# Two gated MLPs after attention: 19 weight quadrants decoded earlier and kept in DRAM, left operands of the second half prepared five steps ahead

## Chip, cores and metric

The kernel runs on one core of a Trainium2 chip. The metric is the device time of one execution in microseconds (us); lower is better.

## What is computed

The inputs are q, k and v of 4 x 12 heads (448 x 64 each), and the weights of two layers. The reference, cut to what matters:

```python
q_n, k_n = rmsnorm(q, g_q), rmsnorm(k, g_k)
scores = np.matmul(q_n, k_n.transpose(0, 1, 3, 2)) / np.sqrt(64)
attn = softmax(scores)                      # with the row maximum taken off
x = heads side by side of attn @ v          # 1792 x 768
x = ((x @ w_a) * (x @ w_b)) @ w_out         # layer 0: 768 -> 1536 -> 768
x = (sigmoid(x @ w_gate) * (x @ w_val)) @ w_out2   # layer 1, same sizes
```

The weights arrive as 64-bit floats, the activations are 32-bit.

## The kernel before

**Matrices in quadrants.** Each matrix product of the two layers is made by a seven-product scheme on a 2 x 2 split (products 1 to 7, `PASSES`): every product needs one left and one right operand that are quadrants or sums and differences of quadrants. Each operand is split into a high and a low part, and each product is three TensorE matmuls (high x high, low x high, high x low).

**Layers in two parts.** `first_part` makes a layer's hidden matrix: 12 blocks of columns m (of w_a and w_b, or w_gate and w_val, in turn) by 7 products p, 84 events (m, p) in the order of the list `orders`, each of 18 matmuls. `second_part` multiplies the gated result with w_out: 7 products by 6 steps f, 42 steps k of 18 matmuls in layer 0. Attention comes first and handles 24 pairs of heads; the first 16 matmul groups of layer 0's first event are mixed into its end (the calls `mlp` in the table `end`, L495).

**Decoding weights.** A weight quadrant comes as 384 KB of 64-bit words into a `raw` tile. `decode` (L633) makes a 128 x 384 tile `d` of 32-bit floats from it: one ScalarE activation (ACT, L639) and three VectorE instructions (DVE, L640, L642, L646). It is a generator with three pauses; after the last instruction it calls `fill`, which issues the load of the next quadrant but one, since two `raw` tiles are kept loaded. `decodes` (L662) walks over a list `plan` of what is to be decoded: "g" entries are the events, four of the seven products of a block need a new quadrant (`NEEDS`); "o" entries are the 24 quadrants of the layer's w_out, which go through tiles d5 and d8 in turn and are stored to DRAM (`wd`), one every 2.3 events from event 24 on. `splits` (L712) forms a product's right operand from the d tiles (L722, L726) and casts it into the tiles wh (ACT, L734) and wl (DVE, L576). `prepare` (L746) advances both generators by one pause per call.

**Who calls prepare.** In attention two calls of `decode` per pair of heads from pair 6 on (L440), each one pause, until the first 8 quadrants and four operands are made. In `first_part` one call per three matmuls, for three events ahead. In the last six steps of layer 0's `second_part` (L1115) for layer 1, whose generator starts with 12 pauses that load four quadrants.

**Left operands.** `operands` (L774) forms the left operands S1 to S4 and A22 of a first part on VectorE (L800, and L576 for xl) and ScalarE (L791 for xh), a piece every 12 matmuls. In the second part `beside` has three generators: `loads` issues the DMAs of gated quadrants (u) and of stored weight quadrants (d), `rights` makes wh and wl (L1026, L1029, L576), `lefts` makes gh and gl (L1044, L1056, L576). Both are kept up to AHEAD = 3 steps ahead of the step that TensorE is given (L1077). The left operands lie in a ring of six tiles.

**Order.** The program order on each engine is the order in which this Python code emits instructions; each engine runs its own list in order. All DMAs named below are issued by the SyncE queue (SP), also in order. A tile name such as d8 with one buffer makes its next writer wait until its last reader, a DMA too, is done.

**Tail of attention.** The table `end` holds, for the last pair (-1) and those before it: x_tr (TensorE transposes into one of three PSUM buffers `tr`), x_out (copies to SBUF, half 0 on ACT, half 1 on DVE, L356 and L358), rsum_tr and rsum_post (the softmax sums through a `tr` buffer and the ACT copy L390 to `row`), the DMAs dr<-row and rs<-dr, norm (L406), put (xd<-xs), and ten calls of `decode` between them.

Of the kernel before, what the change touches and what calls it, by code (L numbers as in the profile page):

```python
# [23 lines left out]
def attention_then_two_gated_mlps(  # L24
# [37 lines left out]
    nc = tc.nc  # L62
# [3 lines left out]
    P = 128  # L66
# [7 lines left out]
    NPAIR = B * NP  # L74
# [11 lines left out]
    HB = DM // 2  # L86
    HF = NF // 2
# [16 lines left out]
    def in_dram(name, cols, *counts):  # L104
        if not counts:
            return dram1.tile([P, cols], F32, tag=name, name=name)
        return [in_dram(f"{name}_{n}", cols, *counts[1:]) for n in range(counts[0])]
# [2 lines left out]
    gd = in_dram("gd", S2, 2, 5, HF)  # L110
    wd = in_dram("wd", HB, 2, 6, HF)
    bd = in_dram("bd", HB, 2, 2, 2)


    def attention():
# [322 lines left out]
            begin_u()  # L438

        def decode(i, n):  # L440
            if i > 5:
                prepare(0, 3, 1)

        def close_s(i):
            sctx.close()
# [84 lines left out]
    AHEAD = 3  # L530
# [3 lines left out]
    EARLY = 4  # L534
# [9 lines left out]
    NS = len(PASSES) * HF  # L544
# [35 lines left out]
        rest(t, hi, lo, eng)  # L580


    def quadrant(l, n, j, q):

        words = layers[l][n].bitcast(U32)
        r, c = q
        if n < 2:
            f = j + HF * c
            return words[HB * r:HB * r + HB, 2 * P * f:2 * P * f + 2 * P].rearrange("(k p) f -> p k f", p=P)
        f = j + HF * r  # L590
        return words[P * f:P * f + P, 2 * HB * c:2 * HB * c + 2 * HB]
# [5 lines left out]
    def weights(l):  # L597

        plan = []
        events = orders[l]  # L600
        k = 0
        for e, (m, p) in enumerate(events):
            plan.append(("g", m, p))
            while k < 4 * HF and e >= 24 + 2.3 * k:
                plan.append(("o", k % HF, (Q11, Q21, Q12, Q22)[k // HF]))
                k += 1
        assert k == 4 * HF
        wanted = [
            (2, m, p) if x == "o" else (m % 2, m // 2, NEEDS[p]) for x, m, p in plan if x == "o" or p in NEEDS
        ]  # L610
        loaded = []
        total = len(wanted)

        def fill():

            while wanted and len(loaded) < (4 if total - len(wanted) < 10 and len(free_u) >= 3 else 2):
                load()

        def load():
            n, j, q = wanted.pop(0)  # L620
            tag = None
            if [t for t, _ in loaded].count(None) >= 2:
                tag, u = take_u()
                r = u[:, 0:2 * HB].bitcast(U32).rearrange("p (f w) -> p f w", w=2)
            else:
                r = rawp.tile([P, HB, 2], U32, tag="raw", name="raw")
            if n < 2:
                nc.sync.dma_start(out=r.rearrange("p (k f) w -> p k (f w)", f=P), in_=quadrant(l, n, j, q))
            else:
                nc.sync.dma_start(out=r.rearrange("p f w -> p (f w)"), in_=quadrant(l, n, j, q))  # L630
            loaded.append((tag, r))

        def decode(t):  # L633
# [27 lines left out]

        def decodes():  # L662
            e = k = -1
            if l == 0:
                fill()
                yield
            else:
                for n in range(12):
                    if n % 3 == 0:
                        load()  # L670
                    yield
            for x, m, p in plan:
                now = stores[:]
                if x == "o":
                    k += 1
                    t = dec("d5" if k % 2 else "d8")
                    yield from decode(t)
                    stores.append((wd[l][QUADS.index(p)][m], t))
                else:
                    e += 1  # L680
                    if p in NEEDS:
                        q = QUADS.index(NEEDS[p])
                        spilled = 2 <= m < EARLY and p < 3
                        tag = f"d{4 * (m % 2) + (q + 1 if spilled else q)}"
                        if q == 1 and m >= EARLY:
                            tag = "d1"
                        if l == 1:
                            while held[0] is not None and tag not in held[0]:
                                yield
                            if held[0] is not None:  # L690
                                held[0].remove(tag)
                        t = dec(tag)
                        B[m, q] = t
                        yield from decode(t)
                        if spilled:
                            stores.append((bd[l][m % 2][q // 2], t))
                for dst, t in now:
                    nc.sync.dma_start(out=dst, in_=t)
                    stores.pop(0)
                decoded[l] = e  # L700
                yield
            for dst, t in stores:
                nc.sync.dma_start(out=dst, in_=t)
            decoded[l] = NE
# [35 lines left out]
        return decodes(), splits()  # L740

    decoded = [-1, -1]

    held = [None]

# [224 lines left out]
    def beside(l):  # L970
# [95 lines left out]
        def step(k, must=False):  # L1066
# [7 lines left out]
                stores()  # L1074
            if len(gl) < 4 and (max(gl) if gl else k) < k + 7:
                next(load, None)
            for d, it in ((WI, right), (GI, left)):  # L1077
                if (max(d) if d else -1) < min(k + AHEAD, NS - 1):
                    next(it, None)

        return step
# [186 lines left out]
```

## Time and profile before

| | us |
|---|---|
| median of 3 runs | 1249.66 (1248.96 to 1249.98) |
| the profiled execution's own time | 1248.36 |
| its span, first to last instruction | 1246.5 |
| TensorE (PE) busy | 1199.8 (96%) |
| VectorE (DVE) busy | 935.9 (75%) |
| ScalarE (ACT) busy | 655.3 (53%) |
| mean granted TensorE clock | 0.991 of full |
| moved by DMA | 203 MB |

Attention takes the stretch to about 284 us, layer 0's first part 284 to 608, its second part 608 to 767, layer 1's first part 768 to 1085, its second part the rest. The views below give each instruction group with its line, its tiles (out<-in) and the time an engine sat idle before it with what it waited for; a stretch of time can be asked for by itself. The time of a matmul is modelled, so two neighbours overlap in the list.

### The profile page before, as it was taken

Reading aid. Unit: us, or ns where it says so; the run is one execution under the profiler, and the core shown is the slowest. Engines: PE = TensorE matmul, PEld = TensorE weight load, DVE = VectorE, ACT = ScalarE, POOL = GpSimd, SP = SyncE. Lnnn points to the kernel's source line nnn. Section 1 sums busy time; section 2 is a strip of 40 time slices with the busy share of each in tenths; the row PEclk is TensorE's granted clock in tenths of the full one; section 3 lists DMA queues with packets and bytes.
Section 4 is the critical chain, followed back from the end, with each engine's and each line's share of the span. In section 5 each row is a group of like instructions: output and inputs, shape, how many; then the busy total and the mean of one; then the engine's idle time right before and its main releaser. Section 6 shows DMA issues by size and latency. Waiting matters only on the chain.

```text
span 1246.5 us, 18142 instructions
## 1 busy us (share of the span) xinstructions
PE 1199.8 (96%) x6414; PEld 1014.0 (81%) x6414; DVE 935.9 (75%) x1621; ACT 655.3 (53%) x1271; POOL 157.0 (13%) x240
## 2 busy tenths in 40 slices
PE   5999999999799999999999999889999999999997
PEld 3666666667688888888888878778888888999997
DVE  6788889874987787876668689966877877557583
ACT  4777787873543544344355556444445344445543
POOL 3656667700000000000000000000000000000000
PEclk9999999999899999999999999999999999999999
DMA  5244455327134565653865753233655654677573
GB/s 130 72 134 127 135 151 160 114 85 253 40 117 148 170 195 153 201 168 113 313 223 160 236 178 119 72 108 119 187 183 161 198 159 155 221 266 252 179 258 101
DMA packets 142025, 202.99 MB, mean 163 GB/s; under 512 B 23240, under 2 KB 116592, under 8 KB 141936
## 3 DMA queue, kind: packets, MB, share of 16 engines
q1 hardware_dynamic: 140496, 201.26, 51.0%
q8 instruction: 50, 0.82, 0.3%
q10 hardware_dynamic: 1440, 0.59, 0.2%
q14 instruction: 39, 0.32, 0.1%
HBM read 147.46 MB, written 54.35 MB: 162 GB/s over the span
## 4 chain that ended last, share of the span: by engine, by line
PE 81%; DVE 10%; ACT 4%; issue 2%; DMA 1%; POOL 1%; ACTq 0%; SPq 0%; DVEq 0%; POOLq 0%
PE mm L887 45%; PE mm L1140 10%; PE mm L1150 9%; PE pv L371 5%; PE s L311 4%; PE tr L342 3%; DVE xl L576 2%; DVE nm L317 2%; PE tr L264 1%; PE tr L339 1%; ACT gh L1056 1%; DVE d L646 1%; DMA d<-wd 1%; DVE wl L576 1%; DVE u L1044 1%
## 5 line engine op out<-in xcount | busy, mean ns | idle before, releaser
L887 PE MATMUL mm<-xh,wh 128*128 128x512 f32 (+1 forms) x1008 | 370.3, 367 | 10.5 <-ACT u L943 4.1
L887 PE MATMUL mm<-xl,wh 128*128 128x512 f32 (+1 forms) x1008 | 370.9, 368 | 5.2 <-DVE xl L576 5.2
L887 PE MATMUL mm<-xh,wl 128*128 128x512 f32 (+1 forms) x1008 | 371.6, 369 | 0.0
L576 DVE TENSOR_TENSOR wl<-d,wh 128x384 fp32r<-128x384 f32 x252 | 140.2, 557 | 158.1 <-ACT wh L734 99.9
L887 PEld LDWEIGHTS mm<-xh,wh 128*128 128x128 f32 x1008 | 190.9, 189 | 36.7 <-ACT u L939 4.5
L887 PEld LDWEIGHTS mm<-xl,wh 128*128 128x128 f32 x1008 | 190.8, 189 | 29.7 <-DVE xl L576 6.9
L887 PEld LDWEIGHTS mm<-xh,wl 128*128 128x128 f32 x1008 | 190.6, 189 | 21.2
L734 ACT CAST wh<-d 128x384 fp32r<-128x384 f32 x168 | 86.1, 513 | 167.8 <-DVE d L722 150.1
L1029 ACT CAST wh<-d 128x384 fp32r<-128x384 f32 x84 | 43.3, 515 | 146.8 <-DVE d L1026 46.5
L639 ACT ACTIVATE d<-raw 128x384 f32<-128x384 f32 x140 | 77.9, 557 | 63.8 <-DMA raw<-in_moe_w_gate_dram 13.9
L329 ACT ACTIVATE P<-s,nm 128x448 f32<-128x448 f32 x168 | 105.3, 636 | 10.3 <-DVE nm L317 9.5
L317 DVE TENSOR_REDUCE nm<-s 128x1 f32<-128x448 f32 x168 | 97.5, 615 | 4.1 <-PE s L311 4.1
L1150 PE MATMUL mm<-wh,gh 128*128 128x384 f32 x294 | 98.8, 336 | 0.6 <-ACT ah L1173 0.3
L1150 PE MATMUL mm<-wl,gh 128*128 128x384 f32 x294 | 98.6, 335 | 0.0
L1150 PE MATMUL mm<-wh,gl 128*128 128x384 f32 x294 | 98.5, 335 | 0.0
L1140 PE MATMUL mm<-gh,wh 128*128 128x512 f32 x252 | 92.6, 367 | 3.1 <-ACT ah L1173 2.9
L1140 PE MATMUL mm<-gl,wh 128*128 128x512 f32 x252 | 93.1, 369 | 0.0
L1140 PE MATMUL mm<-gh,wl 128*128 128x512 f32 x252 | 92.8, 368 | 0.0
L646 DVE SCALAR_TENSOR_TENSOR d<-d,raw 128x384 uint32<-128x384 uint32 x140 | 81.7, 583 | 11.0 <-ACT d L639 1.3
L642 DVE SCALAR_TENSOR_TENSOR raw<-raw 128x384 uint32<-128x384 uint32 x140 | 78.5, 561 | 4.1
L576 DVE TENSOR_TENSOR gl<-u,gh 128x896 fp32r<-128x896 f32 x60 | 65.6, 1093 | 20.0 <-ACT gh L1056 19.9
L358 ACT COPY pt<-tr 128x512 f32<-128x512 f32 x96 | 55.0, 573 | 41.9 <-PE tr L342 38.0
(149 smaller groups left out, 1925.4 us busy)
## 6 DMA issues: line engine op xcount, KB each, us to landing
gd<-u SPq DMA_DIRECT2D x60, 448.0 KB
u<-gd SPq DMA_DIRECT2D x60, 448.0 KB
d<-wd SPq DMA_DIRECT2D x132, 192.0 KB
raw<-in_moe_w_out_dram SPq DMA_DIRECT2D x48, 384.0 KB
wd<-d SPq DMA_DIRECT2D x72, 192.0 KB
raw<-in_moe_w_a_dram SPq DMA_DIRECT2D x24, 384.0 KB
raw<-in_moe_w_b_dram SPq DMA_DIRECT2D x24, 384.0 KB
raw<-in_moe_w_val_dram SPq DMA_DIRECT2D x23, 384.0 KB
```

The costliest lines, as they stand in the source:

```text
L317: nc.vector.tensor_reduce(out=d["nm"][:, t:t + 1], in_=d["ps"][t], axis=AX.X, op=ALU.max, negate=True)
L329: nc.scalar.activation(out=e, in_=d["ps"].pop(t), func=AF.Exp, bias=d["nm"][:, t:t + 1], accum_out=d["sum"][:, t:t + 1])
L358: nc.scalar.copy(out=d["pt"][j][:, w], in_=tr)
L371: nc.tensor.matmul(d["pv"][64 * h:64 * h + 64], w, x, start=(j == 0), stop=(j == R), skip_group_check=True)
L576: eng.tensor_tensor(out=lo, in0=t, in1=f32(hi), op=ALU.subtract)
L639: nc.scalar.activation(out=f32(t), in_=f32(high), func=AF.Copy, scale=2.0 ** -112)
L642: nc.vector.scalar_tensor_tensor(out=low, in0=high, scalar=0x80000000, in1=low, op0=ALU.bitwise_and, op1=ALU.bitwise_or)
L646: nc.vector.scalar_tensor_tensor(out=t, in0=t, scalar=3, in1=low, op0=ALU.logical_shift_left, op1=ALU.bitwise_or)
L734: nc.scalar.copy(out=hi, in_=t)
L887: nc.tensor.matmul(ps[:, o:o + size], w[:, P * c:P * c + P], x[:, o:o + size], start=(p in (1, 5) and c == 0 and z == 0), stop=(c == KC - ...
L1140: nc.tensor.matmul(ps[:, o:o + size], w[:, P * un:P * un + P], g[:, o:o + size], start=(p in (1, 5) and f == 0 and z == 0), stop=(f == HF ...
L1150: nc.tensor.matmul(ps[:, o:o + HB], g[:, P * t:P * t + P], w, start=(p in (1, 5) and f == 0 and z == 0), stop=(f == HF - 1 and z == 2), sk ...
```

## The change

A table of 19 DRAM tiles `pd` holds decoded quadrants: 7 of layer 0 (those that come after its first 8) and the first 12 of layer 1. The 7 are decoded during attention, through the one tile d8, and stored; the 12 are decoded in layer 0's first part, behind its w_out quadrants in the list `extra`, through d5 and d8. Where an event's quadrant is known to be in `pd`, a 192 KB DMA fills its d tile in place of the decode. In attention the calls begin at pair 2 in place of 6; once the first 8 quadrants are made, each call takes one pause of the decoder, two for the last pair, where there are ten calls. In layer 0's first part the extra decodes come every 1.6 events from event 26 on, in place of 2.3 from 24 on. Layer 1's generator starts with a plain `fill`, and the limit of four loaded quadrants holds for layer 0 only. Left operands of both second parts are made up to HF - 1 = 5 steps ahead, right operands 3 as before.

```diff
+    SOON = (7, 12)
+    pd = [in_dram(f"pd{l}", HB, SOON[l]) for l in range(2)]
...
         def decode(i, n):
-            if i > 5:
+            if i > 1 and decoded[0] < 2 * EARLY - 1:
                 prepare(0, 3, 1)
+            elif i > 1:
+                for _ in range(2 if i == NPAIR - 1 else 1):
+                    if left[0]:
+                        next(preps[0][0])
+                    if done[0] < 3:
+                        next(preps[0][1])
...
+    def soon(l):
+
+        first = [(m % 2, m // 2, NEEDS[p]) for m, p in orders[l] if p in NEEDS]
+        return first[2 * EARLY * (1 - l):][:SOON[l]]
...
+        known = {w: n for n, w in enumerate(soon(l))}
+        extra = [("o", k % HF, (Q11, Q21, Q12, Q22)[k // HF]) for k in range(4 * HF)]
+        if l == 0:
+            extra += [("s", 1, w) for w in soon(1)]
+        every = 2.3 if l else 1.6
         for e, (m, p) in enumerate(events):
             plan.append(("g", m, p))
-            while k < 4 * HF and e >= 24 + 2.3 * k:
-                plan.append(("o", k % HF, (Q11, Q21, Q12, Q22)[k // HF]))
-                k += 1
+            if l == 0 and e == 2 * EARLY - 1:
+                plan += [("s", 0, w) for w in soon(0)]
+            while extra and e >= (24 if l else 26) + every * (4 * HF + SOON[1] * (1 - l) - len(extra)):
+                plan.append(extra.pop(0))
...
-            while wanted and len(loaded) < (4 if total - len(wanted) < 10 and len(free_u) >= 3 else 2):
+            while wanted and len(loaded) < (4 if l == 0 and total - len(wanted) < 10 and len(free_u) >= 3 else 2):
                 load()
...
-            if l == 0:
-                fill()
-                yield
-            else:
-                for n in range(12):
-                    if n % 3 == 0:
-                        load()
-                    yield
+            fill()
+            yield
             for x, m, p in plan:
                 now = stores[:]
-                if x == "o":
+                if x == "s" and m == 0:
+                    t = dec("d8")
+                    yield from decode(t)
+                    nc.sync.dma_start(out=pd[0][soon(0).index(p)], in_=t)
+                    left[0] -= 1
+                elif x in "os":
                     k += 1
                     t = dec("d5" if k % 2 else "d8")
                     yield from decode(t)
-                    stores.append((wd[l][QUADS.index(p)][m], t))
+                    stores.append((wd[l][QUADS.index(p)][m] if x == "o" else pd[1][soon(1).index(p)], t))
...
-                        yield from decode(t)
+                        if (m % 2, m // 2, NEEDS[p]) in known:
+                            nc.sync.dma_start(out=t, in_=pd[l][known[m % 2, m // 2, NEEDS[p]]])
+                            yield
+                        else:
+                            yield from decode(t)
...
-            for d, it in ((WI, right), (GI, left)):
-                if (max(d) if d else -1) < min(k + AHEAD, NS - 1):
+            for d, it, n in ((WI, right, AHEAD), (GI, left, HF - 1)):
+                if (max(d) if d else -1) < min(k + n, NS - 1):
```

Three places of the program order follow; line numbers are those of each program's own file.

ScalarE at the tail of attention, from the copy of the last-but-one pair's last transposes on (pt is a copy of transposes, row the softmax sums), before:

```order
L358 COPY pt<-tr 128x448
L358 COPY pt<-tr 128x512 x2
L390 COPY row<-tr 7x128
L358 COPY pt<-tr 128x512
L358 COPY pt<-tr 128x448
```

and with the change:

```order
L360 COPY pt<-tr 128x448
L662 ACTIVATE d_4317<-raw 128x384
L360 COPY pt<-tr 128x512
L662 ACTIVATE d_4347<-raw 128x384
L360 COPY pt<-tr 128x512
L662 ACTIVATE d_4367<-raw 128x384
L662 ACTIVATE d_4385<-raw 128x384
L392 COPY row<-tr 7x128
```

Four decode activations, all into d8, now stand ahead of the copy to row, one to three of them ahead of the copies of transposes.

SP at the same place, with the change (pd is the new table, xd the attention output, dr and rs the softmax sums on their way through DRAM):

```order
L651 DMA raw<-in_moe_w_a_dram 128x3x256
L694 DMA pd_2_237<-d_4176 128x384
L651 DMA raw<-in_moe_w_a_dram 128x3x256
L694 DMA pd_3_238<-d_4317 128x384
L651 DMA raw<-in_moe_w_b_dram 128x3x256
L694 DMA pd_4_239<-d_4347 128x384
L651 DMA raw<-in_moe_w_b_dram 128x3x256
L413 DMA xd_1_4_93<-xs 128x448
L694 DMA pd_5_240<-d_4367 128x384
L394 DMA dr<-row 7x128
```

Each store of a decoded quadrant stands right behind the load of a raw one; none of these loads and stores of weights stood here before, where dr<-row came next after xd_1_4.

VectorE at the start of layer 1's first part (al is a left operand's sum, xl a left low part, wl a right one), before:

```order
L800 TENSOR_TENSOR al<-ah,al 128x896
L640 TENSOR_SCALAR u_8533<-u_8533 128x384
L642 SCALAR_TENSOR_TENSOR u_8533<-u_8533 128x384
L646 SCALAR_TENSOR_TENSOR d_8611<-d_8611,u_8533 128x384
L576 TENSOR_TENSOR wl<-d_8541,wh 128x384
L800 TENSOR_TENSOR al<-ah,al 128x896 x2
L576 TENSOR_TENSOR wl<-d_8566,wh 128x384
L640 TENSOR_SCALAR raw<-raw 128x384
L642 SCALAR_TENSOR_TENSOR raw<-raw 128x384
L576 TENSOR_TENSOR xl<-al,xh 128x896
```

and with the change:

```order
L827 TENSOR_TENSOR al<-ah,al 128x896
L584 TENSOR_TENSOR wl<-d_8615,wh 128x384
L827 TENSOR_TENSOR al<-ah,al 128x896 x2
L584 TENSOR_TENSOR wl<-d_8640,wh 128x384
L584 TENSOR_TENSOR xl<-al,xh 128x896
```

The decode instructions between the left operands' sums are gone here; the order of TensorE's instructions is the same throughout the program.

## Rows read from the trace of the kernel before

**Rows 1.** Page, part 1: busy time, share and instructions of each engine.

```profile
PE 1199.8 (96%) x6414; PEld 1014.0 (81%) x6414; DVE 935.9 (75%) x1621; ACT 655.3 (53%) x1271; POOL 157.0 (13%) x240
```

**Rows 2.** Windows of 25 us: length, busy PE, PEld, DVE, ACT, POOL, PEclk, DMA share, GB/s.

```profile
75.00:100.00 25.00, 25.00 (x174) 16.30 (x174) 20.71 (x48) 18.71 (x54) 15.30 (x23) 1.00 0.53 151
450.00:475.00 25.00, 25.00 (x124) 22.28 (x124) 20.38 (x38) 11.09 (x19) 0.00 (x0) 1.00 0.62 199
```

**Rows 3.** Windows of 15 us at the starts of the two first parts, same columns.

```profile
315.00:330.00 15.00, 10.78 (x46) 8.60 (x45) 14.37 (x19) 8.79 (x13) 0.00 (x0) 0.91 0.21 70
330.00:345.00 15.00, 12.81 (x45) 10.67 (x44) 12.69 (x17) 9.25 (x12) 0.00 (x0) 0.75 0.00 1
810.00:825.00 15.00, 10.92 (x48) 9.41 (x47) 9.12 (x16) 8.62 (x13) 0.00 (x0) 0.89 0.25 82
```

**Rows 4.** Timeline of PE, end of attention and start of layer 0: start, us, instruction, idle before.

```profile
285.03 0.27 PE L344 MATMUL tr<-swap,P 128*128 128x128 f32 x1
...
324.51 0.50 PE L887 MATMUL mm<-xl,wh 128*128 128x512 f32 x1 [1.32 <-DVE xl L576]
...
328.17 0.79 PE L887 MATMUL mm<-xl,wh 128*128 128x512 f32 x1 [2.68 <-DVE xl L576]
...
341.25 0.79 PE L887 MATMUL mm<-xl,wh 128*128 128x512 f32 x1 [0.79 <-DVE xl L576]
```

**Rows 5.** Timelines of DVE and ACT at the tail of attention.

```profile
275.26 0.61 DVE L317 TENSOR_REDUCE nm<-s 128x1 f32<-128x448 f32 x1
280.81 0.25 ACT L390 COPY row<-tr 7x128 f32<-7x128 f32 x1
```

**Rows 6.** Timelines of SP and ACT, and windows around one store and one load with store.

```profile
261.31 0.47 SPq L698 DMA_DIRECT2D bd<-d  x1
...
263.50:264.00 0.50, 0.50 (x4) 0.41 (x4) 0.50 (x2) 0.00 (x0) 0.00 (x0) 1.00 0.00 0
...
780.70 0.38 SPq L628 DMA_DIRECT2D raw<-in_moe_w_val_dram  x1
...
784.46 0.57 ACT L639 ACTIVATE d<-raw 128x384 f32<-128x384 f32 x1 [0.53 <-DMA raw<-in_moe_w_val_dram]
```

**Rows 7.** Instructions of one line, ACT: duration ns min/median/max; page, part 5: DVE L642.

```profile
L639 ACT ACTIVATE d<-raw x140: 538/556/577, 91.0 to 1053.3; 128x384 f32<-128x384 f32 x140
L642 DVE SCALAR_TENSOR_TENSOR raw<-raw 128x384 uint32<-128x384 uint32 x140 | 78.5, 561 | 4.1
```

**Rows 8.** Timeline of DVE, start of layer 0: first sum, one decode, last rest.

```profile
301.64 1.08 DVE L800 TENSOR_TENSOR fl<-fh 128x896 f32<-128x896 f32 x1
302.64 0.36 DVE L640 TENSOR_SCALAR raw<-raw 128x384 uint32<-128x384 uint32 x1
...
303.70 0.56 DVE L646 SCALAR_TENSOR_TENSOR d<-d,raw 128x384 uint32<-128x384 uint32 x1
...
340.11 1.08 DVE L576 TENSOR_TENSOR xl<-fl,xh 128x896 fp32r<-128x896 f32 x1
```

**Rows 9.** Groups of instructions by line, DVE, 395 to 605 us: busy, mean ns, idle before.

```profile
L576 DVE TENSOR_TENSOR wl<-d,wh 128x384 fp32r<-128x384 f32 x58 | 32.2, 557 | 33.6 <-ACT wh L734 32.7 <-PE mm L887 0.7
L640 DVE TENSOR_SCALAR raw<-raw 128x384 uint32<-128x384 uint32 x50 | 17.9, 358 | 10.3 <-DMA raw<-in_moe_w_b_dram 6.5 <-DMA raw<-in_moe_w_out_dram 2.2 <-DMA raw<-in_moe_w_a_dram 1.5
```

**Rows 10.** Timelines of DVE, ACT and PE, layer 0's second part, before its last product.

```profile
732.22 1.08 DVE L1044 TENSOR_TENSOR u<-fl,u 128x896 f32<-128x896 f32 x1
...
743.37 2.51 ACT L1173 COPY ah<-mm 128x896 f32<-128x896 f32 x3
...
744.32 0.79 PE L1140 MATMUL mm<-gh,wh 128*128 128x512 f32 x1 [2.85 <-ACT ah L1173]
```

**Rows 11.** Timeline of PE, start of layer 1's first part.

```profile
796.33 0.50 PE L887 MATMUL mm<-xh,wh 128*128 128x512 f32 x1 [2.77 <-ACT u L939]
...
804.38 0.50 PE L887 MATMUL mm<-xh,wh 128*128 128x512 f32 x1 [0.47 <-ACT mm L861]
...
816.04 0.80 PE L887 MATMUL mm<-xh,wh 128*128 128x512 f32 x1 [4.08 <-ACT u L943]
```

More of the change, by code (lines that the diff above doesn't have):

```diff
@@ L600, in weights @@
         events = orders[l]
-        k = 0
+        known = {w: n for n, w in enumerate(soon(l))}
[3 more added lines that the diff above has]
+        every = 2.3 if l else 1.6
         for e, (m, p) in enumerate(events):
             plan.append(("g", m, p))
-            while k < 4 * HF and e >= 24 + 2.3 * k:
-                plan.append(("o", k % HF, (Q11, Q21, Q12, Q22)[k // HF]))
-                k += 1
[L607 to L610, printed above, removed]
+            if l == 0 and e == 2 * EARLY - 1:
+                plan += [("s", 0, w) for w in soon(0)]
+            while extra and e >= (24 if l else 26) + every * (4 * HF + SOON[1] * (1 - l) - len(extra)):
+                plan.append(extra.pop(0))
+        assert not extra
+        wanted = []
+        for x, m, p in plan:
+            if x == "o":
+                wanted.append((l, 2, m, p))
+            elif x == "s":
+                wanted.append((m, *p))
+            elif p in NEEDS and (m % 2, m // 2, NEEDS[p]) not in known:
+                wanted.append((l, m % 2, m // 2, NEEDS[p]))
         loaded = []
@@ L614, in fill @@
         def fill():
-            while wanted and len(loaded) < (4 if total - len(wanted) < 10 and len(free_u) >= 3 else 2):
+            while wanted and len(loaded) < (4 if l == 0 and total - len(wanted) < 10 and len(free_u) >= 3 else 2):
                 load()
         def load():
-            n, j, q = wanted.pop(0)
+            of, n, j, q = wanted.pop(0)
             tag = None
@@ L627, in load @@
             if n < 2:
-                nc.sync.dma_start(out=r.rearrange("p (k f) w -> p k (f w)", f=P), in_=quadrant(l, n, j, q))
+                nc.sync.dma_start(out=r.rearrange("p (k f) w -> p k (f w)", f=P), in_=quadrant(of, n, j, q))
             else:
-                nc.sync.dma_start(out=r.rearrange("p f w -> p (f w)"), in_=quadrant(l, n, j, q))
+                nc.sync.dma_start(out=r.rearrange("p f w -> p (f w)"), in_=quadrant(of, n, j, q))
             loaded.append((tag, r))
@@ L742, in attention_then_two_gated_mlps @@
     decoded = [-1, -1]
+    left = [SOON[0]]
     held = [None]
```

## The prediction

> **What bounds the kernel now.** I read part 1 of the page first: PE is busy for 1199.8 of the span's 1246.5 us [rows 1], so at most some 47 us can go, and only where PE waits. The windows then say where that is. In the middle of attention and of layer 0's first part PE is busy for all of 25.00 us while DVE has 20.71 and 20.38 us of work [rows 2]: work taken away there is worth nothing, and DVE can take a few us more. In the first 30 us of layer 0 it is the other way round: PE has 10.78 and 12.81 us of work in two stretches of 15, DVE 14.37 and 12.69, and PE is granted 0.91 and 0.75 of its clock [rows 3]. The waits inside name one cause, the low parts xl of the left operands that DVE has not yet made: 1.32, 2.68 and 0.79 us [rows 4]. The price of such a wait is more than itself: behind it the matmul takes 0.79 us, where it took 0.50 ahead of it [rows 4], that is, it runs at the lower of the two clock levels for some us. Layer 1's first part begins in the same way, with waits of 2.77, 0.47 and 4.08 us [rows 11] and a granted clock of 0.89 [rows 3]. One more wait of 2.85 us, also with 0.79 us behind it, stands before layer 0's last product, for ACT's copy ah [rows 10]. Between these places PE is fed.
>
> The sum below is made against the profiled execution's own 1248.36 us. The median of the runs is 1.30 above it, so I add 1.30 at the end.
>
> **Part 1: twelve quadrants of layer 1 decoded in layer 0 instead (faster, 8.5 us).** A decode is 0.56 us on ACT [rows 7] and 0.36 + 0.56 + 0.56 = 1.5 us on DVE [rows 7, 8]. All twelve leave the stretch around the border of the layers: seven before 771.5 us, five in the 35 us behind it, which takes 7.5 us from DVE ahead of 806. Of these DVE regains about six on the last left operand, whose sum now ends near 809 us instead of 815, as I get by walking through DVE's and ACT's new order with the old durations; PE needs it at 809.9. The waits of 2.77, 0.47 and 4.08 = 7.32 us would go. The clock of 0.89 over 15 us is 3.3 us at the half level, a loss of 1.65 at most, of which I take 1.35. That makes 8.7; I take 8.5 and the bounds 6 and 9. The lower one leaves the wait for ACT (2.77, "u L939"), which no decode causes. In return twelve loads of 192 KB from pd come onto SP; they are issued a decode ahead of their use, and the DMA share is 0.25 there [rows 3].
>
> **Part 2: the same twelve in the middle of layer 0 (slower, 0.5 us).** There they come to 36 entries, one every 1.6 events, where 24 stood one every 2.3. It adds about 1.9 us of DVE to each 25 us, 22.3 instead of 20.4 [rows 2]. What DVE waits for there is seldom the decode: 33.6 us for ACT's wh, 10.3 for raw loads in 210 us [rows 9]. Since the right operands are still prepared three events ahead, I take 0.5; the bounds are 0, and 4 if one raw load in each window of 25 us (eight of them) comes 0.5 us too late, which is 10.3 us over 50 decodes [rows 9] doubled and then half of it reaching PE.
>
> **Part 3: seven quadrants of layer 0 decoded in attention; their gain (faster, 4.0 us).** Four decodes, 6 us of DVE, leave the chain from the first left sum at 301.64 to the last low part at 340.11 [rows 8]. Not all comes back: with the decodes gone DVE waits for ACT's casts, which stand behind PE's result copies, and the walk gives holes of about 1.9 us. The last low part then ends at 337.0 instead of 341.2: 4.2, taken as 4.0. The bounds: 1.5, where only the waits of 0.79 and its clock go, and 7, where all the idle time of the 30 us, 4.22 + 2.19 [rows 3], and a little of the clock goes.
>
> **Part 4: their cost (slower, 11.3 us).** The first eight quadrants are now finished some pairs earlier, in pairs where PE has no idle time and DVE has 4.3 us free in 25 [rows 2]; that costs nothing. The seven need 7 x 3 pauses more. Counting the calls of the table, one per pair up to pair 22 and twenty in the last one, three are decoded ahead of the tail and the last four in the tail. All go through one tile, d8, and each is stored from it. So ACT's activation of the next quadrant, the first write to d8, waits until the store of the last one has landed, and behind that activation stand, in ACT's order, the copies of the transposes and the copy to row. This wait is not in the trace of before; the nearest rows bound it. A store of the same size alone, issued at 261.31, has no DMA traffic left by 263.5 [rows 6]: 2.2 us, 2.6 with the 0.4 us in which SP issues the raw load that stands ahead of each of these stores. A raw load that was issued at 780.70 let ACT go on at 784.46 [rows 6]: 3.7 us. With ACT's 0.56 and DVE's last 0.56 us [rows 7, 8] one quadrant goes round in 3.7 to 4.8 us. The third quadrant's last DVE instruction ends 1.6 us behind the row maximum at 275.26 [rows 5], at 276.9; four stores in a row at 4.8 bring the seventh activation to 295.0 and the copy to row to 295.8, instead of 280.81 + 0.25 [rows 5]. PE's transposes at 285.03 [rows 4] need the tr buffer that this copy frees, so they come 10.7 us later; by the shorter cycle 6.5. I take 10.0, near the longer one, because there too a load and a store share the queues. What stands behind shifts alike: the softmax sums' way through DRAM, the last stores of x, and the first left sum at 301.64, whose inputs have 3 to 5 us in hand and so arrive with PE. PE then stands still for longer than in any row here, and after the waits of 2.68, 2.85 and 4.08 its matmuls took 0.79 to 0.80 [rows 4, 10, 11]; I add 1.3 for the clock, as layer 1's entry lost, with 2.5 as the upper end. The bounds are 6.5 and 13.2 as long as this wait decides.
>
> The Trainium skill, page "DMA: Bandwidth & Descriptors", section "Anatomy of one DMA — SWDGE (gpsimd) path", has a rule that speaks against storing and then waiting: a transfer costs about 2.0 us fixed, most of it the receipt of the write at its target, DRAM being the dearest, and only then its bytes at 436 GB/s. By it 192 KB take 2.45 us (an estimate from that page), the cycle about 4.05, the wait about 7.7 instead of 10.0, and the time would be some 2.3 lower than the sum below; the 2.2 us of the store alone agree with it, the 3.7 of load and store are longer.
>
> **Part 5: left operands five steps ahead (faster, 2.4 us).** In layer 0's second part the subtraction L1044, 1.08 us on DVE [rows 10], and the casts behind it come two steps earlier, out of the steps in which ACT and DVE also make final results. PE's 2.85 us wait for ah at 744.32 would shrink to about 1.1, since ACT reaches the copy at about 741.65 instead of 743.37 [rows 10], and part of the slow matmuls behind it goes too. Bounds: 0, and 4.0 with wait and clock gone. The ring has six tiles, so the operand of step k + 5 is written when PE has done step k - 1; that was done long before.
>
> **Sum.** - 8.5 + 0.5 - 4.0 + 11.3 - 2.4 = - 3.1: 1245.3 against the profiled execution, 1246.6 against the median. About 0.2% (2.5 us) is what a measurement of this kernel tells from no change.
>
> **Rivals.** *The tail costs little.* If the stores land early enough, or the copies of attention's last pair had slack, then what is left of part 4 is about half of its lower end of 6.5: 1249.66 - 8.5 + 0.5 - 4.0 - 2.4 + 3.2 = 1238.5. For it speaks the store of 2.2 us; against it, that even the short cycle delays the copy to row by more than 6 us, and it has no other way round. I give it 14%, all faster.
>
> *The decodes taken away only become other waits (the slower side).* At layer 0's entry DVE's chain may be held by ACT's casts of wh and xh, and these by PE's own results that ACT copies in between. Then the removed 6 us turn into idle time of DVE, part 3 is worth 0, and layer 1's entry, where the longest waits name ACT's u [rows 11], gives 5 instead of 8.5: 11.3 + 0.5 - 2.4 - 5.0 = + 4.4, 1254.1. For it speaks that DVE is not full in the second stretch of layer 0 (12.69 of 15) and waits 33.6 us for wh later [rows 3, 9]; against it, that PE's waits there name DVE's xl [rows 4]. It decides if the last low part of layer 0 comes less than 1 us nearer to the first sum. I give it 28%; 24 of them slower, 4 within 0.2%.
>
> *The seven stay outside the tail.* If the quadrants were all stored ahead of the last pair, part 4 would be nothing; the emitted order puts four activations ahead of the copy to row, so this has no chance of its own.
>
> **How the numbers follow.** The forecast has the remaining 58%. Its own range, from part 4's ends and the walk's bounds, is about 1242 to 1251; 34 of the 58 lie below 1247.1 and count as faster, 24 as the same. Faster is 34 + 14 = 48%, the same 24 + 4 = 28%, slower 24%. The range from 1240 to 1254 leaves out most of the first rival and the upper half of the second, about 2 in 10.
>
> **What would show it.** Part 4: in the profile after, ACT's decode activations near 280 to 296 us wait for the DMA pd<-d, PE's last transposes wait 8 to 11 us for ACT's copy to row, and the matmuls behind take 0.79. Part 3: the stretch from the first left sum to the last low part is 4 us shorter. Part 1: the three waits at layer 1's entry are gone and the clock there is 1.00. Part 5: the wait for ah is about 1 us. Part 2: PE stays at 25.00 of 25 in layer 0's middle. The prediction is wrong if PE idles in layer 0's middle, if the tail's wait is under 5 us, or if layer 1's entry keeps waits of over 3 us.

## The result, and the profile after

The changed kernel takes 1267.3 us (median of 4 runs, 1266.8 to 1268.3), the kernel before 1249.8 beside it: a ratio of 1.0141 (95% interval 1.0124 to 1.0159), 17.5 us slower. The forecast was 1246.6, with 1254 as the upper end.

The page of the changed kernel, its first lines, which answer to [rows 1]:

```profile
span 1265.0 us, 18267 instructions
## 1 busy us (share of the span) xinstructions
PE 1204.1 (95%) x6414; PEld 1014.5 (80%) x6414; DVE 933.4 (74%) x1621; ACT 655.6 (52%) x1271; POOL 157.7 (12%) x240
```

The engines' instruction counts are the same (the loads and stores of pd are added on SP). Of the 18.5 us by which the span grew, only 4 are PE's own busy time; the rest is waiting. As PE runs the same instructions in the same order in both kernels, the two timelines of PE can be laid side by side: the start of one matmul after, minus its start before, is what has been lost up to it.

| stretch, by its last matmul before -> after | shift at its end | the stretch | predicted |
|---|---|---|---|
| attention, to 279 us | -0.7 | -0.7 | 0 |
| attention's tail, 286.62 -> 301.30 | +14.7 | +15.3 | +11.3 |
| layer 0's entry, 345.75 -> 359.28 | +13.5 | -1.2 | -4.0 |
| layer 0's middle, 564.69 -> 583.38 | +18.7 | +5.2 | +0.5 |
| layer 0's second part, 747.82 -> 768.55 | +20.7 | +2.0 | -2.4 |
| layer 1's entry, 821.34 -> 837.93 | +16.6 | -4.1 | -8.5 |
| the rest, 1239.02 -> 1257.26 | +18.2 | +1.6 | 0 |

Every term but attention's is on the bad side of its forecast. **The tail first.** Timeline of ACT in the changed kernel:

```profile
280.65 0.55 ACT L662 ACTIVATE d<-raw 128x384 f32<-128x384 f32 x1 [3.64 <-DMA pd<-d]
...
286.11 0.55 ACT L662 ACTIVATE d<-raw 128x384 f32<-128x384 f32 x1 [4.43 <-issue]
...
291.59 0.55 ACT L662 ACTIVATE d<-raw 128x384 f32<-128x384 f32 x1 [4.46 <-DMA pd<-d]
297.57 0.55 ACT L662 ACTIVATE d<-raw 128x384 f32<-128x384 f32 x1 [5.43 <-DMA pd<-d]
298.02 0.24 ACT L392 COPY row<-tr 7x128 f32<-7x128 f32 x1
```

Four activations stand ahead of the copy to row; three name the store out of d8, and the second, which the view puts down to "issue", follows the same pattern. SP's timeline has a raw load and the store ahead of it:

```profile
281.82 0.38 SPq L651 DMA_DIRECT2D raw<-in_moe_w_a_dram  x1
282.25 0.48 SPq L694 DMA_DIRECT2D pd<-d  x1
```

The raw data of this activation's own quadrant was there by then, for DVE's timeline shows it at work on it:

```profile
282.71 0.55 DVE L665 SCALAR_TENSOR_TENSOR raw<-raw 128x384 uint32<-128x384 uint32 x1
```

PE waits for what stands behind them, in its timeline:

```profile
281.73 0.55 PE L344 MATMUL tr<-ident,P 128*128 128x128 f32 x3 [2.15 <-ACT pt L360]
...
287.18 0.47 PE L341 MATMUL tr<-ident,P 128*128 128x128 f32 x1 [4.05 <-ACT pt L360]
...
298.31 0.47 PE L346 MATMUL tr<-swap,P 128*128 128x128 f32 x1 [5.14 <-ACT row L392]
...
299.29 0.78 PE L914 MATMUL mm<-xh,wh 128*128 128x512 f32 x1
```

**Layer 0's middle** has three waits of a kind that was not there before, all for the ACT copy that puts earlier sums into a PSUM bank:

```profile
502.83 0.50 PE L914 MATMUL mm<-xh,wh 128*128 128x512 f32 x1 [1.25 <-ACT mm L888]
...
556.07 0.50 PE L914 MATMUL mm<-xh,wh 128*128 128x512 f32 x1 [1.07 <-ACT mm L888]
...
583.38 0.50 PE L914 MATMUL mm<-xh,wh 128*128 128x512 f32 x1 [1.40 <-ACT mm L888]
```

Ahead of the third of them, in ACT's timeline, the copy stands behind a decode activation that waits for its raw quadrant:

```profile
581.97 0.56 ACT L662 ACTIVATE d<-raw 128x384 f32<-128x384 f32 x1 [1.32 <-DMA raw<-in_moe_w_b_dram]
582.44 0.89 ACT L888 COPY mm<-u 128x896 f32<-128x896 f32 x1
```

ACT's groups by line, 350 to 610 us, of the kernel before and then of the changed one, say how long ACT waited for raw quadrants: 65.2 us instead of 29.4.

```profile
L639 ACT ACTIVATE d<-raw 128x384 f32<-128x384 f32 x59 | 32.9, 557 | 29.4 <-DMA raw<-in_moe_w_a_dram 13.2 <-DMA raw<-in_moe_w_b_dram 11.0 <-DMA raw<-in_moe_w_out_dram 4.3
```

```profile
L662 ACT ACTIVATE d<-raw 128x384 f32<-128x384 f32 x69 | 38.7, 561 | 65.2 <-DMA raw<-in_moe_w_b_dram 25.4 <-DMA raw<-in_moe_w_a_dram 18.0 <-DMA raw<-in_moe_w_out_dram 11.9
```

**The second part and layer 1's entry**, PE's timeline, answering to [rows 10, 11]: the wait for ah is 2.58 instead of 2.85, the wait for al ahead of it is 1.59 (0.26 before), and of layer 1's three waits one of 3.02 is left.

```profile
695.44 0.50 PE L1167 MATMUL mm<-gh,wh 128*128 128x512 f32 x1 [1.59 <-ACT al L1192]
...
764.93 0.50 PE L1167 MATMUL mm<-gh,wh 128*128 128x512 f32 x1 [2.58 <-ACT ah L1200]
...
832.38 0.50 PE L914 MATMUL mm<-xh,wh 128*128 128x512 f32 x1 [3.02 <-ACT u L970]
```

### The profile page after: what moved, and what is told of

The parts are those of the page before. It is cut to its first block, busy times and chain, and to the rows that moved or that the text cites. A ratio compares the mean times of both kernels' runs of the same rounds, so it can differ in the third digit from the quotient of the medians.

```text
span 1265.0 us, 18267 instructions
## 1 busy us (share of the span) xinstructions
PE 1204.1 (95%) x6414; PEld 1014.5 (80%) x6414; DVE 933.4 (74%) x1621; ACT 655.6 (52%) x1271; POOL 157.7 (12%) x240
## 4 chain that ended last, share of the span: by engine, by line
PE 43%; DVE 5%; ACT 4%; issue 2%; DMA 2%; ACTq 0%; SPq 0%; DVEq 0%
PE mm L914 26%; PE mm L1167 10%; PE mm L1177 8%; ACT gh L1083 1%; DVE u L1071 1%; DMA raw<-in_moe_w_a_dram 1%; DVE xl L584 1%; DMA u<-gd 1%; DVE d L1053 1%; DVE wl L584 0%; DVE al L827 0%; DMA raw<-in_moe_w_b_dram 0%; DVE d L748 0%; DVE d L669 0%; DVE u L938 0%
## 5 line engine op out<-in xcount | busy, mean ns | idle before, releaser
L663 DVE TENSOR_SCALAR raw<-raw 128x384 uint32<-128x384 uint32 x144 | 56.3, 391 | 32.7 <-DMA raw<-in_moe_w_b_dram 10.6
```

What stands on the lines that cost most here:

```text
L663: nc.vector.tensor_scalar(out=low, in0=low, scalar1=29, scalar2=None, op0=ALU.logical_shift_right)
```

## The experiments

Times of the kernel before in the same sessions were 1249.1 to 1249.5; e runs start from the changed kernel, the others as their texts say. The diffs show the lines that matter; "..." stands for others.

**Lead alone taken back (e1_lead3), and alone put in (g3_lead5).**

```diff
-            for d, it, n in ((WI, right, AHEAD), (GI, left, HF - 1)):
+            for d, it, n in ((WI, right, AHEAD), (GI, left, AHEAD)):
```

> The changed kernel with the left operands three steps ahead again, as before the change; nothing else. Theory: the five-step lead puts two more left operands in ACT's and DVE's order ahead of PE's result copies, and costs 1.8 us in layer 0's second part and 1.7 in layer 1's; so this run is 2 to 4 us faster than the changed kernel (1267.3), and the waits of PE for the copies al and ah are those of the kernel before (0.26 and 2.85). Rival, the prediction's part 5: the lead is worth 2.4 us and something else costs the 3.5; then this run is about 2 us slower than the changed kernel.

> The kernel before with the left operands five steps ahead, and nothing else of the change. Theory: two more left operands stand in ACT's order ahead of the copies al and ah of PE's results; by the traces that is worth -0.3 us in layer 0's second part and +1.3 in layer 1's: 1250.5, 1 us over the kernel before. Rival, the prediction: -2.4, 1247.

Without the lead: 1264.2 us in the median, 3.1 less, but the four runs lie in two pairs, near 1266.4 and near 1261.9, so the size is uncertain. The trace is from the upper pair: in it the wait for al is gone from PE's timeline and the last one for ah is 3.15, yet layer 0's second part gives next to nothing back: more matmuls behind that last wait run at the lower clock level than in the changed kernel (granted clock 0.77 against 0.89 from 760 to 775 us). Layer 1's second part does give its 1.6 us back. Put into the kernel before: 1251.5, ratio 1.0020 (1.0011 to 1.0028), so the lead by itself costs 2 us. Its waits of PE are those of the changed kernel:

```profile
677.60 0.50 PE L1140 MATMUL mm<-gh,wh 128*128 128x512 f32 x1 [1.59 <-ACT al L1165]
...
747.36 0.50 PE L1140 MATMUL mm<-gh,wh 128*128 128x512 f32 x1 [2.60 <-ACT ah L1173]
...
1198.18 0.45 PE L1150 MATMUL mm<-wh,gh 128*128 128x384 f32 x1 [0.98 <-ACT ah L1169]
```

The theory held in direction, and its size was under the mark in layer 0: 1.3 us more at al and a new wait of 0.58 for ah, not a gain of 0.3.

**The seven left out (e2_no7), finished before the tail (e3_pairs), or through two tiles (e4_tiles).**

```diff
-    SOON = (7, 12)
+    SOON = (0, 12)
```

> The changed kernel without the seven quadrants decoded in attention (the twelve stay). Theory: the wait at the tail, 15.1 us by the shift of PE between 280 and 300 us, goes whole, and layer 0's entry loses the 1.2 us that the seven gained; 1253.4 us, about 14 faster than the changed kernel, 3.5 over the kernel before. Rival: part of the tail's delay is not in the stores (later copies, clock, the first sum's inputs); then less than 10 us come back.

```diff
-            if i > 1 and decoded[0] < 2 * EARLY - 1:
-                prepare(0, 3, 1)
-            elif i > 1:
-                for _ in range(2 if i == NPAIR - 1 else 1):
+            for _ in range(0 if i < 2 else 1 if n == 0 and i < NPAIR - 1 else 2):
+                if decoded[0] < 2 * EARLY - 1:
+                    prepare(0, 3, 1)
+                else:
                     if left[0]:
...
```

> The changed kernel with all seven quadrants finished ahead of the last pair: three pauses of a decode per pair of heads from pair 2 on instead of two and then one, so that no decode is left at attention's tail. Theory: the decodes are free where PE is full and DVE is not, only their place at the tail costs; 1267.3 - 15.1 = 1252 us, and PE stays at 25.00 of 25 in the pairs; layer 0's entry keeps its 1.2 us, so it is about 1 us faster than the run without the seven. Rival: three pauses per pair fill DVE and PE idles in the pairs; then it is 3 us or more slower than the run without the seven.

```diff
-                    t = dec("d8")
+                    t = dec("d1" if left[0] % 2 else "d8")
```

> The changed kernel with the seven quadrants going through two tiles in turn (d8, and d1 which is free by then) instead of d8 alone; their place at the tail is unchanged. Theory: ACT's wait is for the store out of the one tile; with two tiles each store has a whole decode more, the copy to row comes near 286.5 us instead of 298.0, and the time is 10 to 12 us under the changed kernel (1256). Rival: the pace at the tail is set by the loads of raw quadrants, two at a time; then the activations still come 5 us apart, and it gains under 4 us.

Without the seven: 1250.7 us, ratio 1.0015 (1.0005 to 1.0024). They cost 16.6 us, which the traces account for: 15.3 at the tail, less 1.2 at the entry, plus 2.3 that attention gained when they went. With two tiles: 1255.4, 11.9 under the changed kernel, and the copy to row comes at 287.38, near the 286.5 expected. ACT's timeline:

```profile
281.18 0.56 ACT L662 ACTIVATE d<-raw 128x384 f32<-128x384 f32 x1 [2.81 <-DMA pd<-d]
...
284.18 0.55 ACT L662 ACTIVATE d<-raw 128x384 f32<-128x384 f32 x1 [1.97 <-DMA pd<-d]
286.91 0.56 ACT L662 ACTIVATE d<-raw 128x384 f32<-128x384 f32 x1 [2.18 <-DMA pd<-d]
287.38 0.24 ACT L392 COPY row<-tr 7x128 f32<-7x128 f32 x1
```

So the wait is the store out of the one tile, as predicted: the activations come 2.7 to 3.0 us apart, not 5. The tail is not free even so; 3.2 of its 15.3 us are left.

The third run (e3_pairs) was a miss that taught something: nothing is left at the tail, yet it takes 1255.6, 5 us more than without the seven. Its PE loses in the pairs. The windows 200 to 250 us of the kernel before, of this run, and of f1_pair2 below (PE's busy time is the second number):

```profile
200.00:250.00 50.00, 46.31 (x317) 29.50 (x318) 44.90 (x95) 39.28 (x105) 35.71 (x48) 1.00 0.45 133
```

```profile
200.00:250.00 50.00, 45.20 (x308) 28.82 (x305) 44.16 (x92) 38.61 (x104) 36.26 (x46) 1.00 0.47 141
```

```profile
200.00:250.00 50.00, 48.50 (x331) 30.80 (x328) 44.22 (x97) 41.00 (x110) 37.24 (x51) 1.00 0.44 130
```

The rival's number came, but DVE is no fuller in e3_pairs than in f1_pair2 (44.16 and 44.22 us of 50). PE waits for ACT's copies of the transposes, in whose list the decode activations stand too; that these are what delays the copies was not tested by itself. PE's waits from 75 to 279 us (total, times, longest), f1_pair2, then e3_pairs; the kernel before has 4.1 us of them:

```profile
PE tr L339 <- ACT pt L358: 2.1, 4, 1.0
```

```profile
PE tr L341 <- ACT pt L360: 7.1, 8, 1.1
```

**Earlier decodes in attention alone (f1_pair2)**, on the kernel before.

```diff
-            if i > 5:
+            if i > 1:
                 prepare(0, 3, 1)
```

> The kernel before with one thing of the change: attention's decodes of the first eight quadrants begin at pair 2 instead of pair 6, so that none is left in the last pairs; nothing is stored early and nothing else moves. Theory: a decode costs PE 0.4 to 0.5 us a pair in pairs 18 to 23, where GpSimd makes low parts beside it, and nothing in pairs 2 to 5; in the run without the seven, attention was 2.6 us shorter, so this run is 2.6 us under the kernel before (1246.5). Rival: those 2.6 us came from something else of the change; then this run is the kernel before within 1 us.

1247.1 us, ratio 0.9980 (0.9971 to 0.9989): the theory holds. Laid beside the kernel before, PE is level until 215 us and then gains 0.6 us by 225 and 1.8 more by 250, around the places where the kernel before decodes (ACT's activations at 221.9 and 244.9 us). In the changed kernel the seven fill the late pairs again and this gain does not show.

**Layer 0's middle: a third raw tile (f2_raw3), fewer decodes (f4_soon5).** Both without the seven.

```diff
-  ... and len(free_u) >= 3 else 2):
+  ... and len(free_u) >= 3 else 3 if l == 0 and len(wanted) < total - 12 and len(free_u) >= 3 else 2):
```

> The changed kernel without the seven, and with a third raw quadrant kept loaded in layer 0's first part, in a u tile, where three are free. Theory: the 36 extra decodes are late there because two raw tiles allow one decode per about 2.8 us, load latency and decode together, and ACT, which waits for the raw data, holds PE's result copies; the 7.3 us that layer 0's first part lost in the run without the seven fall to 2 or less, 1245 us. Rival: DVE is the limit there (its 1.5 us for each decode), or the DMA bandwidth; then a third buffer changes under 2 us and it stays at 1249 to 1251.

```diff
+    SOON = (0, 5)
+        every = 2.3 if l else 2.0
```

> The changed kernel without the seven, with five quadrants of layer 1 decoded in layer 0 instead of twelve (29 extra entries there, one every 2.0 events), and left operands three steps ahead. Theory: the loss in layer 0's first part (7.3 us with 36 entries every 1.6 events) is from the decodes' pace and falls to under 2; layer 1's entry keeps most of its 4.9 us, since five decodes had lain in its chain; attention keeps 2.6: 1244 us. Rival: layer 1's gain needs all twelve; then the seven left decodes delay the first sum and it is about 1249.

f4_soon5 also sets the left operands' lead back to three, as its text says. The third tile: 1250.3 us, the rival's number, but not the rival's reason. In the middle PE's waits are gone (its shift stays at +3.1 from 365 to 608 us); ACT's groups, 350 to 610 us:

```profile
L662 ACT ACTIVATE d<-raw 128x384 f32<-128x384 f32 x47 | 26.1, 555 | 19.6 <-DMA raw<-in_moe_w_a_dram 10.2 <-DMA raw<-in_moe_w_b_dram 5.3 <-issue 2.2
L662 ACT ACTIVATE d<-u 128x384 f32<-128x384 f32 x24 | 13.3, 553 | 0.8 <-DMA u<-in_moe_w_b_dram 0.4 <-DMA wd<-d 0.4
```

That is 20.4 us of waits instead of 65.2. What it won there it lost ahead of 365 us, where the left operands need the u tile that it took: PE's shift goes from -2.1 to +3.1, by waits such as this one.

```profile
335.08 0.79 PE L914 MATMUL mm<-xh,wh 128*128 128x512 f32 x1 [3.78 <-ACT xh L818]
```

Five instead of twelve: 1247.5 us, ratio 0.9982, and PE is busy for 225.00 of 225 us from 395 to 620; but layer 1's entry gains nothing (PE's shift is -1.3 ahead of it and -1.1 behind), so that five are not enough for it, as the rival said; numbers between five and twelve were not run. Of the 3.2 us under the run without the seven, about 2 are the lead's (g3_lead5).

**Layer 1's entry: wl on GpSimd (f3_wlpool, g2_simple, h1_tiles_wl).** f3 without the seven, g2 on f1_pair2's edit with no quadrant moved, h1 on e4_tiles for layer 0. The edit is f3's; in g2 the condition is `l == 1 and e < 14`, in h1 `l == 0 and 3 < e < 14`.

```diff
-                rest(t, hi, lo, nc.vector)
+                rest(t, hi, lo, nc.gpsimd if e < 14 else nc.vector)
```

> The changed kernel without the seven, and with the low parts wl of the first 14 events of each first part made by GpSimd instead of DVE. Theory: at the layers' entries DVE's decodes had filled the time in which its next instruction, wl, waits for ACT's cast wh, which stands behind the copy of PE's result; where the decodes are gone the wait shows (4.2 us of holes in layer 1), and the left operands' sums queue behind it. With wl on GpSimd these holes close: layer 1's last low part comes 3 to 4 us earlier and PE's wait of 3.0 us there is gone, layer 0's entry gains 2 to 4 more; about 5 us under the run without the seven (1246). Rival: the sums wait for something else (their casts xh behind the same PE copies, or wl is late from GpSimd), and it gains under 1 us or loses.

> The kernel before with attention's decodes from pair 2 on and the low parts wl of layer 1's first 14 events on GpSimd; the twelve decodes stay at layer 1's border. Theory: DVE's chain at layer 1's entry has hardly any holes as long as the decodes fill them, so taking wl off it frees 0.5 us a piece, and PE's waits there fall by 2 to 3 of 7.3 us: 1244.5. Rival: the wait is for DVE's own work of decodes and sums, and each wl less counts fully with the clock: 1242 or less, and then the twelve need not move at all.

> The run with the two tiles (1255.4), and the low parts wl of layer 0's events 4 to 13 on GpSimd. Theory: the three decodes that left DVE's chain at layer 0's entry came back as waits of wl for ACT's wh, so the chain from the first left sum to the last low part went from 38.5 to 36.25 us only; with wl off DVE it is 33 to 34 us, and PE's waits of 2.57 and 1.67 there shrink by 2 to 3: 1253. Rival: the chain is bound by ACT's casts xh, which stand behind the same copies; it stays over 35.5 us and the time within 1 us of 1255.4.

Why wl: in the changed kernel DVE's timeline at this entry shows waits where the decodes had been, 2.10 + 1.11 + 0.95 us, each for ACT's cast wh, which in ACT's order follows a copy of PE's result.

```profile
793.84 0.56 DVE L584 TENSOR_TENSOR wl<-d,wh 128x384 fp32r<-128x384 f32 x1 [2.10 <-ACT wh L760]
...
797.51 0.56 DVE L584 TENSOR_TENSOR wl<-d,wh 128x384 fp32r<-128x384 f32 x1 [1.11 <-ACT wh L760]
...
801.14 0.56 DVE L584 TENSOR_TENSOR wl<-d,wh 128x384 fp32r<-128x384 f32 x1 [0.95 <-ACT wh L760]
```

f3: 1248.0 us, 2.7 less than without the seven; the first sum starts at 770.13 us instead of 775.81 and PE's wait is 1.90 instead of 3.01. Layer 1's entry gains 1.5 us more by PE's shift than without the edit, short of the theory's 3 to 4; in layer 0 nothing was won. The holes did not close: where DVE had waited for wh, its low parts xl now wait for the casts xh (3.82, 1.35 and 1.37 us for the first three), as the rival said, and the chain from the first sum to the last low part is 41.5 us, against 39.6 without the edit. It starts earlier by 5.7 us, where PE itself is 2.3 us earlier, and that is what is left of the gain. g2: 1247.8, no gain over f1_pair2's 1247.1. Its first wait grew to 5.00 us (2.77 before), its last fell to 2.63: the two parts need each other. h1: 1254.0, 1.4 under e4_tiles, which the spread of the two does not tell from nothing, and DVE's chain from 306.3 to the last low part's start at 340.87 became 306.5 to 340.70. The waits for wh are gone from it, but the first sum waits for its input in both runs (fh<-xd), and in h1 some sums take longer beside GpSimd:

```profile
312.72 1.18 POOL L584 TENSOR_TENSOR wl<-d,wh 128x384 fp32r<-128x384 f32 x1 [3.18 <-ACT wh L760]
```

```profile
313.05 1.80 DVE L827 TENSOR_TENSOR fl<-fl 128x896 f32<-128x896 f32 x1
...
328.44 1.89 DVE L827 TENSOR_TENSOR fl<-fl,fh 128x896 f32<-128x896 f32 x1
```

For layer 0's entry that test leaves open how much of the lost gain was the waits for wh alone.

**What the runs favour, together (g1_best):** no seven, the twelve, decodes from pair 2, lead three, wl of layer 1's first 14 events on GpSimd, and the third raw tile from event 26 on:

```diff
+  ... else 3 if l == 0 and decoded[0] >= 26 and len(free_u) >= 3 else 2):
```

> What the runs so far favour, together: no quadrants for layer 0 from attention (and its decodes from pair 2 on), the twelve of layer 1, a third raw quadrant in layer 0's first part from event 26 on, the low parts wl of layer 1's first 14 events on GpSimd, left operands three steps ahead. Theory: attention -3, layer 0's entry 0, layer 0's middle 0 (the third raw tile takes the 7 us away when it does not take a u tile from the entry), second part 0, layer 1's entry -8: 11 us under the kernel before, 1238.5. Rival: DVE, with 22 of 25 us of work in layer 0's middle, is the limit there and 3 us or more of the 7 stay; 1242 or more.

1239.0 us (1238.1 to 1239.4), ratio 0.9913 (0.9898 to 0.9929): 10.5 us under the kernel before. By PE's shift attention gives -2.6, layer 0's entry +1.1, its middle 0.0, its second part +0.2 and layer 1's entry -7.3. Its windows show layer 0's middle full and layer 1's entry nearly so:

```profile
350.00:610.00 260.00, 260.00 (x1279) 232.05 (x1278) 208.20 (x379) 112.69 (x196) 0.00 (x0) 1.00 0.62 197
766.00:830.00 64.00, 62.13 (x305) 55.14 (x304) 46.85 (x56) 33.47 (x48) 12.59 (x11) 1.00 0.20 65
```

## Why the prediction was wrong, step by step

The forecast was -3.1 us and PE's timeline says +18.2. The difference of some 21 us is 4.0 at the tail, 2.8 at layer 0's entry, 4.7 in its middle, 4.4 in its second part, 4.4 at layer 1's entry and 1.6 in the rest, less 0.7 in attention: no single term made it wrong. Two of the prediction's own signs of being wrong came: PE idles in layer 0's middle, and layer 1's entry keeps a wait of over 3 us (3.02).

**Part 4, the tail: mechanism right, size wrong.** The third quadrant's store, the activation at 280.6 and the chain up to the copy to row came as described. The term mis-sized was "3.7 us" from the raw load's issue until ACT goes on: the runs show 4.3, 4.3 and 4.8 (281.82 to 286.11, 287.27 to 291.59, 292.76 to 297.57). The row I took as the longer bound is the landing of the load, the first of two transfers (in that place too SP issues a store 0.43 us behind it, at 781.13); here ACT waits for the store, the second of the two, and another store of x stood between the third pair. The row for the shorter bound was misread as well: that store was not alone, a 192 KB load of v had been issued at 260.89, and 2.2 us is the end of the traffic, not the moment at which a waiter goes on. The cycle is 5.5 to 6.0 instead of 4.8. PE was 13.9 us late at the transposes, not 10.0, and lost 1.4 by the clock behind them, as taken (1.3). The bound of 13.2 was no bound. The Trainium skill, page "DMA: Bandwidth & Descriptors", section "Anatomy of one DMA — SWDGE (gpsimd) path", gave 2.45 us for a store of this size (the estimate in the prediction). Its fit is for one transfer issued from GpSimd, while these stores go out on SP behind a load; the trace shows 3.9 from the store's own issue until ACT goes on (282.25 to 286.11), and for this case the measurement decides.

**Part 3, layer 0's entry: -1.2 instead of -4.0.** "Four decodes leave the chain from 301.64 to 340.11" was a miscount: in the timeline before three lie inside it (at 302.64, 305.65 and 321.85 us), 4.4 us. The waits of about 1.9 us that I expected came (1.10 and 0.83 for wh and PE). The chain went from 38.5 to 36.25 us:

```profile
316.30 2.09 DVE L827 TENSOR_TENSOR fl<-fh 128x896 f32<-128x896 f32 x2
...
352.55 1.08 DVE L584 TENSOR_TENSOR xl<-fl,xh 128x896 fp32r<-128x896 f32 x1
```

Half of the 2.2 won was lost again. PE's last wait there ends with a shift of 12.4 (341.25 -> 353.69), but behind it the matmuls take 0.80 us, at the lower clock level (granted clock 0.77 from 350 to 365 us), for 5.6 us against 3.2 before, and at 345.75 -> 359.28 the shift is 13.5. The waits that came in place of the decodes are what the second rival described; by its own sign, a last low part less than 1 us nearer, it did not decide, since that came 2.2 us nearer.

**Part 2, layer 0's middle: +5.2 instead of +0.5.** I judged it by DVE's busy time, which rose by 10 us in 250, about half of what I took, and stayed under 25 in each 25 us (same stretch of PE's work, the kernel before and the changed one):

```profile
350.00:600.00 250.00, 250.00 (x1230) 223.02 (x1229) 186.06 (x333) 105.17 (x179) 0.00 (x0) 1.00 0.52 164
```

```profile
363.50:613.50 250.00, 246.16 (x1204) 217.92 (x1203) 195.78 (x359) 107.96 (x186) 0.00 (x0) 1.00 0.60 183
```

The resource that ran out was the pair of raw tiles: each is refilled only when its decode is done, and the load takes some 3.5 to 4 us (one issued at 577.92 let ACT go on at 581.97). The runs settle it: from 365 to 608 us e2_no7 loses 7.0 us with two tiles, f2_raw3 and g1_best lose nothing with the same decodes and a third tile (PE has 260.00 of 260 in g1_best), and f4_soon5 nothing with two tiles and fewer decodes.

**Part 5, the lead: +2.0 in layer 0's second part, and +2.0 in the whole when put in alone, instead of -2.4.** The step that failed is "ACT reaches the copy at about 741.65 instead of 743.37": the wait for ah stayed at 2.58. I moved the operand casts ahead of the finals in my walk and forgot that the casts of still later steps then stand ahead of the copies al and ah. In the changed kernel a cast gh stands right ahead of the copy ah, as one did before (742.52 us, with the copy at 743.37):

```profile
763.14 0.93 ACT L1083 CAST gh<-u 128x896 fp32r<-128x896 f32 x1
763.98 2.52 ACT L1200 COPY ah<-mm 128x896 f32<-128x896 f32 x3
```

Layer 1's second part uses the same code; I gave it no term, and it cost 1.6. All traces with a lead of five lose 1.1 to 3.1 us there, none with a lead of three loses any.

**Part 1, layer 1's entry: -4.1 instead of -8.5.** "Of 7.5 us DVE regains about six" is the step. The chain from the first sum to the last low part before PE's last wait went from 42.4 us (771.50 to 813.90) to 39.6 (790.65 to 830.24): of the 7.4 us removed, 4.6 were not won, 4.2 of them because of longer waits for wh. Before, then with the change:

```profile
771.50 1.08 DVE L800 TENSOR_TENSOR al<-ah,al 128x896 f32<-128x896 f32 x1
...
813.90 1.09 DVE L576 TENSOR_TENSOR xl<-u,xh 128x896 fp32r<-128x896 f32 x1
```

```profile
790.65 1.08 DVE L827 TENSOR_TENSOR al<-ah,al 128x896 f32<-128x896 f32 x1
...
830.24 1.09 DVE L584 TENSOR_TENSOR xl<-u,xh 128x896 fp32r<-128x896 f32 x1
```

My walk of the new orders missed that each wh in ACT's list waits behind a copy of PE's result, which comes no earlier for a free DVE. The term of 1.35 for the clock gave nothing either: the granted clock is 0.89 from 825 to 840 us, as it was from 810 to 825 before.

**The rivals.** The first, a tail that costs little, is out: the copy to row came at 298.02 instead of 280.81. The slower one named the mechanism for parts 1 and 3, and in its rest kept my terms for the tail, the middle and the lead; so it gave 1254, not 1267. That decodes ahead of the tail are free was right from pair 2 on at two pauses a pair up to about 200 us (f1_pair2); it is wrong at three pauses (e3_pairs) and for the late pairs, where the kernel before has PE busy for 46.31 of 50 us. [rows 2] showed one earlier window, 75 to 100 us, and I took it for all.

## What to carry to other kernels

Work moved off a full engine is only a gain where the instruction behind it can start: walk both in-order engines, the one that loses the work and the one that releases its next instruction. Where work moves into a stretch that has room, ask for its buffers' round trip (load, use, refill) and not only for the engine's busy time. A tile that is written, stored and written again in one queue makes the store's landing part of the compute path; here a second tile took 12 of 15 us away.

## What the runs showed of the hardware that was not expected

A 192 KB store issued 0.43 us behind a 384 KB load let ACT go on 3.9 us after its own issue (282.25 to 286.11). Behind a 192 KB load, a store of the same size left no traffic 2.2 us after its issue [rows 6]; the first is an end of waiting and the second an end of traffic, so the two cannot be set against each other directly.

In h1_tiles_wl five DVE sums of two tiles took 1.79 to 1.91 us instead of 1.08 where a GpSimd subtraction ran beside them, and GpSimd's subtractions beside DVE took 1.18 to 1.64 instead of 1.02. The sum at 313.05 ends 1.08 us after about 313.8, when GpSimd's (312.72, 1.18 us) was nearly done. The Trainium skill, page "SBUF — State Buffer", section "SBUF: two separate sides", says that such a pair shares ports, and that whichever starts first holds them for its whole instruction while the other waits; the trace agrees for this pair, with 0.72 us of waiting.
